# 384-column spatial halves, contiguous transposes, paired causal products and shifted scheduler ranks in a delta-rule, gMLP and rotor kernel

## Chip, cores and metric

The kernel runs on one core of one Trainium2 chip. The metric is the device time of one execution in microseconds (us); less is better. Engines are TensorE (PE, its weight loads PEld), VectorE (DVE), ScalarE (ACT), GpSimd (POOL) and SyncE (SP), whose queue issues all transfers.

## The reference

Three stages follow one another, all in float32, with B = 4 batches, H = 8 heads, S = 768 positions, D = 48.

```python
for t in range(S):                                  # stage 1a: delta rule, k_n = k / |k|
    y[:, :, t] = einsum('bhd,bhde->bhe', q[:, :, t], state)
    v_old = einsum('bhde,bhd->bhe', state, kt)
    state = state + bt * einsum('bhd,bhe->bhde', kt, vt - v_old)
x = y as [B, S, H * D = 384]
u, v = split(maximum(x @ w_in, 0))                  # stage 1b: gMLP, 512 columns each
v_n = (v - mean) / sqrt(var + 1e-6)
v_s = einsum('ts,bsd->btd', w_spatial, v_n) + b_spatial
x = (u * v_s) @ w_out                               # stage 2: rotor
theta = x @ w_theta
y = einsum('ts,bsd->btd', w_tok_r, x * cos(theta)) + einsum(..., w_tok_i, x * sin(theta))
z = x + y;  out = z + maximum(z @ w_ch, 0)
```

## The kernel before

Every instruction is a task with a rank (its priority), a cost in ns on each engine that may run it, and the buffers that it reads and writes. `Plan.run` is a list scheduler: it walks through a modelled time and emits on each engine the task that can start first, among those that can start at once the one of lowest rank. What it emits is the fixed order of each engine's queue. Large matmul groups are tasks marked `big`; in `pe_pick` they fill TensorE while the recurrence waits. Where a gap in the model would let TensorE's clock fall, the planner puts in filler transposes of the identity (`filler`, L529), up to `FILL_K` = 8 for one gap, and 60 once at the start.

Stage 1a. The 48 chunks (4 batches of 12, 64 positions each) are one serial recurrence. `chain(g)` (L831) does, with rank g: products with the state S (`fr`, L854) and a subtraction on VectorE (`rt`, L857); a product with the inverted triangular matrix (`fu`, L866), copied out as U; the update of S (`fs`, L878), copied out; then the output y (`fy`, L902), with rank g + 0.5, added up in `xs` (L913) and stored. `fr`, `fu` and `fy` share one PSUM tile, `ru`, so the next `fr` waits for the add at L913. `jit(g)` (L787) makes the masked product of k and q for a chunk: on PSUM tile `m` for the first 12 chunks, then on `gp` with one mask product of 256 elements on VectorE (L811). The triangular matrices of 8 chunks at a time (a round, six in all) are made by `gram2` and inverted by `invert(r)` (L666): a mask product in place in GX (L678, not in round 0), a 32x32 transpose from GX into `un` (L688), a norm, 30 steps of elimination with a product and an add each (L727, L738), a product with gaT (L741), two more transposes (L744 in place in `un`, L747 back into GX), and small matmuls (L765, L771). There is one buffer of `un`.

Stage 1b. Each float32 matmul of this and the next stage is three (high x high, high x low, low x high parts). For each batch `m_V` projects 128 positions at a time to 512 columns and normalises; `m_U` makes u transposed, 256 positions at a time; `m_S(b, h3, fp)` (L1113) makes the spatial product for 256 positions (h3 of three) and two groups of 128 features, which lie side by side in one PSUM tile: 2 x 18 matmuls of 256 columns. VectorE adds the bias (L1128) and multiplies with u (L1131), 512 elements each, and the tile `gt`, of which there are two, is stored to DRAM (L1133). There are two PSUM tiles `m`. All matmuls of `mm_tasks` carry line 1012. Weights of stage 2 are meanwhile converted and parked in DRAM (`park`, L1181).

Stage 2 opens its PSUM when the recurrence has ended. For each of 24 tiles of 128 positions: reload of the gated product every second tile (`load_g`, L1283: two pieces of 512 columns, split into high and low parts in the single buffers `gh` and `gl`), `X2`, a transpose `T2`, `TH`, sine and cosine, and 36 matmuls of 384 columns (`Y`); the output per batch in `U2` and `O`.

```python
r_gt = ring("w3", "gt", [128, 2, TG], F32, 2)                      # L959
k = max(min(need, FILL_K), min(room, more))                        # L370, fillers for a gap
```

## Time and profile before

| | us |
|---|---|
| median of 3 runs | 736.78 (736.3 to 739.08) |
| profiled execution | 740.0 |
| its span, first to last instruction | 738.2 |
| TensorE busy | 688.6 (93%) |
| VectorE busy | 553.8 (75%) |
| ScalarE busy | 358.6 (49%) |

The span is from the first to the last instruction of the profiled execution, whose own time is a little longer. Busy time is the union of an engine's instructions. [...] The profile's page gives busy time per engine, the same in 40 slices, and the costliest groups of instructions; the trace gives each stretch, group and instruction. After a wait, `<-` names what ended it. Matmuls are pipelined, so the distance between their starts, not the length of one, is what a stream costs.

### The profile page before, as it was taken

To read this page: it belongs to the slowest core of one execution; us is meant where nothing else is said; L and a number is where in the kernel's file an instruction comes from. 1 tells how busy PE (TensorE), PEld (TensorE's weight loads), DVE (VectorE), ACT (ScalarE), POOL (GpSimd) and SP (SyncE) were. 2 spreads that over 40 slices of the span, in tenths; PEclk is the share of its full clock that TensorE was granted. 3 is DMA by queue.
4 is the path that set the end of the run, shared out by engine and by line. 5 is a ranking of instruction groups with operands and counts; after the bars stand their busy time and mean duration, and the time that the engine had idled before them with its cause. 6 is when DMAs were issued, how large, how long until landed. Compare 5 with 4: busy or idle time off the path is not lost. (4 is left out here: it accounts for less than half of the span.)

```text
span 738.2 us, 23758 instructions
## 1 busy us (share of the span) xinstructions
PE 688.6 (93%) x10048; PEld 636.9 (86%) x10048; DVE 553.8 (75%) x1530; ACT 358.6 (49%) x874; POOL 12.4 (2%) x18
## 2 busy tenths in 40 slices
PE   5585988799998999999989999999999999999997
PEld 4575676599886798888889899999999999999997
DVE  7999999959989999857756868776555746574555
ACT  5755484543366762367754764564232423332331
POOL 0010010000010000100000000000000000000000
PEclk9995899879999999999999999999999999999999
DMA  8434634415457535667687543530100011011001
GB/s 300 146 113 125 188 107 127 137 39 154 151 161 213 176 89 160 172 214 230 198 257 273 159 145 128 168 115 30 65 29 28 29 65 30 29 29 65 0 1 65
DMA packets 67786, 90.65 MB, mean 123 GB/s; under 512 B 6624, under 2 KB 46432, under 8 KB 67680
## 3 DMA queue, kind: packets, MB, share of 16 engines
q1 hardware_dynamic: 67680, 89.14, 39.0%
q8 instruction: 79, 1.29, 0.7%
q14 instruction: 27, 0.22, 0.1%
HBM read 66.70 MB, written 22.41 MB: 121 GB/s over the span
## 5 line engine op out<-in xcount | busy, mean ns | idle before, releaser
L1012 PE MATMUL m<-w,vh 128*128 128x256 f32 x576 | 112.5, 294 | 2.7 <-DVE gt L1128 2.7
L1012 PEld LDWEIGHTS m<-w,vh 128*128 128x128 f32 x576 | 90.1, 193 | 6.1 <-DVE gt L1128 3.0
L1012 PE MATMUL y<-wr,xTh 128*128 128x384 f32 x432 | 86.5, 338 | 0.0
L1012 PE MATMUL y<-w,xTl 128*128 128x384 f32 x432 | 84.7, 338 | 0.0
L1012 PE MATMUL m<-w,vl 128*128 128x256 f32 x288 | 81.9, 284 | 0.2 <-DVE vl L943 0.2
L1012 PEld LDWEIGHTS y<-wr,xTh 128*128 128x128 f32 x432 | 75.8, 188 | 0.0
L1012 PEld LDWEIGHTS y<-w,xTl 128*128 128x128 f32 x432 | 75.4, 188 | 0.0
L738 DVE TENSOR_TENSOR un<-un,tmp 128x30 f32<-128x30 f32 (+21 forms) x209 | 60.7, 301 | 1.5
L727 DVE TENSOR_TENSOR tmp<-un 128x30 f32<-128x30 f32 (+21 forms) x209 | 60.5, 300 | 1.5
L1012 PEld LDWEIGHTS m<-w,vl 128*128 128x128 f32 x288 | 55.7, 193 | 0.4 <-DVE vl L943 0.4
L1340 DVE TENSOR_SCALAR bgr<-m 128x384 int32<-128x384 f32 x22 | 12.2, 556 | 56.1 <-PE m L1012 56.1
L497 ACT ACTIVATE U<-ru 128x96 f32<-128x96 f32 x75 | 14.8, 248 | 66.4 <-PE ru L866 49.2
L1012 PE MATMUL m<-xTh,wih 128*128 128x256 f32 x144 | 46.4, 322 | 0.4 <-ACT hv L497 0.4
L1012 PE MATMUL m<-wo,gh 128*128 128x384 f32 x176 | 44.7, 334 | 0.0
L497 ACT ACTIVATE x<-m 128x384 f32<-128x384 f32 x14 | 6.8, 489 | 74.3 <-PE m L1012 74.3
L1012 PE MATMUL m<-xTl,wih 128*128 128x256 f32 x144 | 41.9, 291 | 0.0
L1012 PE MATMUL m<-xTh,wil 128*128 128x256 f32 x144 | 41.7, 290 | 0.0
L1012 PE MATMUL m<-uh,wc 128*128 128x384 f32 x144 | 38.3, 335 | 0.0
L497 ACT ACTIVATE bgr<-bgr 128x384 uint8<-128x384 uint8 x34 | 36.6, 1075 | 0.5
L1012 PE MATMUL m<-wt,xh 128*128 128x384 f32 x132 | 33.8, 337 | 0.0
L1012 PE MATMUL m<-wih,xTh 128*128 128x512 f32 x72 | 33.2, 461 | 0.4 <-ACT xTh L497 0.3
L1354 DVE TENSOR_TENSOR bgr<-x,bgr 128x384 f32<-128x384 f32 x48 | 25.9, 553 | 9.6 <-ACT bgr L497 9.2
(186 smaller groups left out, 1647.0 us busy)
## 6 DMA issues: line engine op xcount, KB each, us to landing
kq<-in_kqT_dram SPq DMA_DIRECT2D x48, 256.0 KB, 3.6
vk<-in_vkn_dram SPq DMA_DIRECT2D x48, 192.0 KB, 3.0
kg<-in_kgT_dram SPq DMA_DIRECT2D x24, 256.0 KB, 3.4
gd<-gt SPq DMA_DIRECT2D x24, 256.0 KB, 3.0
graw<-gd SPq DMA_DIRECT2D x24, 256.0 KB, 2.8
xd<-xs SPq DMA_DIRECT2D x48, 96.0 KB, 2.9
xr<-xd SPq DMA_DIRECT2D x24, 192.0 KB, 3.0
bgr<-in_w_r_dram SPq DMA_DIRECT2D x12, 384.0 KB, 4.5
```

The costliest lines, as they stand in the source:

```text
L497: nc.scalar.activation(out=out, in_=in_, func=func, **kw)
L727: nc.vector.tensor_tensor(out=t3, in0=un.t[:, k:k + 1, 0:k].to_broadcast([128, m, k]), in1=un.t[:, t0:32:st, k:k + 1].to_broadcast([128, m ...
L738: nc.vector.tensor_tensor(out=un.t[:, t0:32:st, 0:k], in0=un.t[:, t0:32:st, 0:k], in1=t3, op=ALU.add)
L1012: mm(out=view(), lhsT=a, rhs=c, start=(start and q == 0 and s_ == 0), stop=(stop and q == tot - 1 and s_ == 2))
L1340: P.add(o_dve(DM), lambda e: nc.vector.tensor_scalar(out=ni.t.bitcast(I32), in0=th(), scalar1=1.0 / TWO_PI, scalar2=None, op0=ALU.mult), [ ...
L1354: P.add(o_tts(DM), lambda e, src=src: eng[e].tensor_tensor(out=src.t, in0=x2.t, in1=src.t, op=ALU.mult), [x2], [src], pr)
```

## The change

- `m_S` takes 384 positions (h of two) and one group of 128 features: 18 matmuls of 384 columns in one PSUM tile, 8 tiles per batch where there were 6. The bias add has 384 elements; the product with u is cut at the borders of the 256-position tiles of u, into pieces of 256 and 128. `gt` has 384 columns and three buffers. The gated product lies in DRAM in pieces of 384 columns; `load_g` reads it in pieces of 256 or, across the border of a half, twice 128, with four buffers, and splits it 256 columns at a time.
- In `invert`, the mask product writes `un` in transposed order and the first transpose is in place and contiguous (not in round 0). The product with gaT writes GX, again in another order, and the second transpose reads GX without a stride along its blocks.
- `jit` from chunk 12 on makes the products of two chunks in one task and masks them with one VectorE instruction of 512 elements.
- S and U have 16 zero columns more, so `fy` loads 64 columns as weights and writes all rows; two memsets of `ru` go, four small ones on GpSimd come.
- `fu` of chunk g is ordered behind `fy` of chunk g - 2.
- At most 4 fillers for one gap. The ranks of four runs of tasks are shifted by fixed pseudo-random offsets (`NUDGE`: seed, first task, last task, size). `STAY` is 0 and does nothing; modelled costs of the transposes are new.

```diff
-FILL_K = 8
+FILL_K = 4
...
+STAY = 0.0
+NUDGE = ((9376, 863, 1113, 0.3), (6411, 2108, 2228, 0.6), (938, 2559, 2679, 0.6), (1081, 1922, 2422, 0.3))
+TRB = 1900.0
+SPER = 6
+GTN = 3
...
+        for k, lo, hi, amp in NUDGE:
+            r = random.Random(k)
+            for t in self.tasks[lo:hi]:
+                t.prio += r.uniform(-amp, amp)
...
-    St = [pools["pa"].tile([128, HP, D], F32, name=f"S{i}") for i in range(2)]
-    Ut = [pools["pa"].tile([128, HP, D], F32, name=f"U{i}") for i in range(2)]
+    St = [pools["pa"].tile([128, HP * D + 16], F32, name=f"S{i}") for i in range(2)]
+    Ut = [pools["pa"].tile([128, HP * D + 16], F32, name=f"U{i}") for i in range(2)]
...
-    r_jp = ring("pa", "jp", [128, HP, CH], F32, JPN)
+    r_jp = ring("pa", "jp", [128, 2 * HP, CH], F32, JPN)
...
         if not cr:
             A([("DVE", d_dve(1024))], lambda e: nc.vector.tensor_tensor(
-                out=gx[:, :, 0:32], in0=gx[:, :, 0:32], in1=mask2.t.unsqueeze(1).to_broadcast([128, 32, 32]), op=ALU.mult),
-              G + [mask2, gg[1], gg[3]], gm2, pr)
-        un = r_un.new()
+                out=un.t.rearrange("p t u -> p u t"), in0=gx[:, :, 0:32], in1=mask2.t.unsqueeze(1).to_broadcast([128, 32, 32]), op=ALU.mult),
+              G + [mask2, gg[1], gg[3]], [un], pr)
+
...
-            nc.vector.transpose(out=un.t, in_=gx[:, :, 0:32].rearrange("p u t -> p t u"))
-
-        A([("DVE", 1900.0)], f1, G + [gg[1], gg[3]] + gm2, [un], pr, crit=cr, port=False)
+            nc.vector.transpose(out=un.t, in_=gx[:, :, 0:32].rearrange("p u t -> p t u") if cr else un.t)
+
+        A([("DVE", 1960.0 if cr else 1180.0)], f1, G + [gg[1], gg[3]], [un], pr, crit=cr, port=False)
...
         A([("DVE", d_dve(1024))], lambda e: nc.vector.tensor_tensor(
-            out=un.t, in0=un.t, in1=gt.t.unsqueeze(1).to_broadcast([128, 32, 32]), op=ALU.mult), [un, gt], ub, pr + 0.05, crit=cr)
+            out=gx[:, :, 0:32].rearrange("p s t -> p t s"), in0=un.t, in1=gt.t.unsqueeze(1).to_broadcast([128, 32, 32]), op=ALU.mult),
+          [un, gt] + ub, gg, pr + 0.05, crit=cr)
         xt = Buf()
-        A([("DVE", 1900.0)], lambda e: nc.vector.transpose(out=un.t.rearrange("p u s -> p s u"),
-                                                           in_=un.t.rearrange("p t s -> p s t")),
-          ub, [xt, un], pr + 0.05, crit=cr, port=False)
-        A([("DVE", 1900.0)], lambda e: nc.vector.transpose(out=gx[:, :, 0:32], in_=un.t), [xt, un], gg, pr + 0.1, crit=cr, port=False)
+        A([("DVE", TRB)], lambda e: nc.vector.transpose(out=un.t.rearrange("p u s -> p s u"), in_=gx[:, :, 0:32]),
+          gg, [xt, un], pr + 0.05, crit=cr, port=False)
+        A([("DVE", 1250.0)], lambda e: nc.vector.transpose(out=gx[:, :, 0:32], in_=un.t), [xt, un], gg, pr + 0.1, crit=cr, port=False)
...
+        elif g % 2 == 0:
-            pj = [lambda: GPt[:, 384:512], lambda: GPt[:, 512:640]]
...
+            jp = jp_b[g] = jp_b[g + 1] = r_jp.new()
+            A(o_pe(2 * JPE), f, [kq_b[g], kq_b[g + 1]], pss + [jp], pr, after=grams if r < 2 else (), act=0.55)
+            A(o_dve(512), lambda e: nc.vector.tensor_tensor(
+                out=jp.t, in0=GPt[:, 256:768].rearrange("p (h t) -> p h t", t=CH), in1=mask.t[:, 0].unsqueeze(1).to_broadcast([128, 8, CH]), op=ALU.mult),
+              [pss[0], mask], [jp], pr, port=False, after=inv0)
...
+        marks[g].order.update(ys_b[-2:-1])
...
-                        lh, rh = s[i:i + D, SB[hp], :], kq.t[i:i + D, 1, hp, :]
+                        lh, rh = s[i:i + D, D * SB[hp]:D * SB[hp] + 64], kq.t[i:i + D, 1, hp, :]
                     else:
-                        lh, rh = u[i:i + 64, UB[hp], :], jp.t[i:i + 64, SB[hp], :]
-                    mm(out=PYv[h][o:o + D, c0:c0 + CH], lhsT=lh, rhs=rh, start=f, stop=w == 1 or UF[hp] > 0, skip_group_check=True)
+                        lh, rh = u[i:i + 64, D * UB[hp]:D * UB[hp] + 64], jp.t[i:i + 64, SB[hp] // 2 * 4 + (g % 2 * 2 if g >= JM else 0) + SB[hp] % 2, :]
+                    mm(out=PYv[h]()[o:o + 64, c0:c0 + CH], lhsT=lh, rhs=rh, start=f, stop=w == 1 or UF[hp] > 0, skip_group_check=True)
...
-    r_gt = ring("w3", "gt", [128, 2, TG], F32, 2)
...
+    r_gt = ring("w3", "gt", [128, HALF], F32, GTN)
...
-    def m_S(b, h3, fp, pr):
+    def m_S(b, h, f, pr):
-        v3 = (lambda: ps.t.rearrange("p (f t) -> p f t", t=TG))
-        t0, t1 = h3 * TG, (h3 + 1) * TG
-        for ff in range(2):
-            f0, f1 = (2 * fp + ff) * 128, (2 * fp + ff + 1) * 128
-            gr = [lambda i=i, f0=f0, f1=f1: (vh_b[b, i].t[:, f0:f1], vl_b[b, i].t[:, f0:f1], ws_h[i].t[:, t0:t1], ws_l[i].t[:, t0:t1])
-                  for i in range(NT)]
-            mm_tasks(ps, lambda ff=ff: v3()[:, ff, :], gr, TG, [[vh_b[b, i], vl_b[b, i], ws_h[i], ws_l[i]] for i in range(NT)],
-                     pr, per=UPER)
-        gt, u, gd = r_gt.new(), uT_b[b, h3], gdram[b][fp][h3]
-        if fp == 0:
-            bs_b[b, h3] = r_bs.new()
-            load(bs_b[b, h3], lambda t=bs_b[b, h3]: t.t, b_sp[:, t0:t1], 131072, pr)
-        bs = bs_b[b, h3]
-        P.add(o_dve(2 * TG), lambda e: nc.vector.tensor_tensor(
-            out=gt.t, in0=v3(), in1=bs.t.unsqueeze(1).to_broadcast([128, 2, TG]), op=ALU.add),
+        t0, f0, f1 = h * HALF, f * 128, (f + 1) * 128
+        gr = [lambda i=i: (vh_b[b, i].t[:, f0:f1], vl_b[b, i].t[:, f0:f1], ws_h[i].t[:, t0:t0 + HALF], ws_l[i].t[:, t0:t0 + HALF])
+              for i in range(NT)]
+        mm_tasks(ps, lambda: ps.t[:, 0:HALF], gr, HALF, [[vh_b[b, i], vl_b[b, i], ws_h[i], ws_l[i]] for i in range(NT)], pr, per=SPER)
+        gt, gd = r_gt.new(), gdram[b][f][h]
+        if f == 0:
+            bs_b[b, h] = r_bs.new()
+            load(bs_b[b, h], lambda t=bs_b[b, h]: t.t, b_sp[:, t0:t0 + HALF], 196608, pr)
+        bs = bs_b[b, h]
+        P.add(o_dve(HALF), lambda e: nc.vector.tensor_tensor(out=gt.t, in0=ps.t[:, 0:HALF], in1=bs.t, op=ALU.add),
-        P.add(o_tts(2 * TG), lambda e: eng[e].tensor_tensor(out=gt.t, in0=gt.t, in1=u.t[:, 2 * fp:2 * fp + 2, :], op=ALU.mult),
-              [u], [gt], pr)
-        stores.add(P.add(dma(262144), lambda e: nc.sync.dma_start(out=gd.t, in_=gt.t), [gt], [gd], pr, extra=2000.0))
+        t = t0
+        while t < t0 + HALF:
+            n = min(t0 + HALF, (t // TG + 1) * TG) - t
+            u = uT_b[b, t // TG]
+            P.add(o_tts(n), lambda e, u=u, t=t, n=n: eng[e].tensor_tensor(
+                out=gt.t[:, t - t0:t - t0 + n], in0=gt.t[:, t - t0:t - t0 + n], in1=u.t[:, f, t % TG:t % TG + n], op=ALU.mult),
+                  [u], [gt], pr)
+            t += n
+        stores.add(P.add(dma(196608), lambda e: nc.sync.dma_start(out=gd.t, in_=gt.t), [gt], [gd], pr, extra=2000.0))
...
+        for h in range(2):
+            for f in range(KF):
+                m_S(b, h, f, pr)
...
-        for f in range(KF // 2):
-            raw, gd = r_gr.new(), gdram[b][f][h3]
-            P.add(dma(262144), lambda e, raw=raw, gd=gd: nc.sync.dma_start(out=raw.t, in_=gd.t), [gd], [raw], pr, extra=LOADLAT)
-            split(raw, lambda raw=raw: raw.t, 2 * TG, gh, lambda f=f: gh.t[:, 2 * f:2 * f + 2], gl, lambda f=f: gl.t[:, 2 * f:2 * f + 2], pr)
+        t0 = h3 * TG
+        for f in range(KF):
+            raw = r_gr.new()
+            t = t0
+            while t < t0 + TG:
+                h = t // HALF
+                n, gd = min(t0 + TG, (h + 1) * HALF) - t, gdram[b][f][h]
+                P.add(dma(512 * n), lambda e, raw=raw, gd=gd, t=t, n=n, h=h: nc.sync.dma_start(
+                    out=raw.t[:, t - t0:t - t0 + n], in_=gd.t[:, t - h * HALF:t - h * HALF + n]), [gd], [(raw, t > t0)], pr, extra=LOADLAT)
+                t += n
+            split(raw, lambda raw=raw: raw.t, TG, gh, lambda f=f: gh.t[:, f], gl, lambda f=f: gl.t[:, f], pr)
```

## Rows read from the trace of the kernel before

**Rows 1.** The page's 40 slices of the span, busy tenths of VectorE.
```profile
DVE  7999999959989999857756868776555746574555
```

**Rows 2.** Stretches: us; busy by engine (instructions); granted clock (PEclk); DMA share, GB/s.
```profile
0.00:276.00 276.00, 234.00 (x5761) 200.74 (x5762) 249.60 (x817) 157.27 (x433) 10.39 (x14) 0.91 0.49 148
140.00:144.00 4.00, 1.93 (x6) 0.97 (x6) 3.93 (x6) 0.14 (x2) 0.00 (x0) 0.99 0.43 158
144.00:160.00 16.00, 15.78 (x275) 14.18 (x277) 8.87 (x26) 7.30 (x18) 2.25 (x2) 0.58 0.20 55
232.00:244.00 12.00, 8.30 (x263) 6.87 (x263) 11.93 (x42) 7.87 (x22) 0.00 (x0) 0.95 0.74 229
276.00:460.00 184.00, 180.51 (x2698) 163.49 (x2697) 134.62 (x366) 103.36 (x235) 2.04 (x4) 0.99 0.63 194
384.00:394.00 10.00, 7.30 (x46) 6.98 (x45) 7.69 (x16) 5.48 (x8) 0.00 (x0) 0.83 1.03 382
460.00:738.00 278.00, 274.07 (x1593) 272.69 (x1591) 169.56 (x349) 97.99 (x207) 0.00 (x0) 1.00 0.16 51
```

**Rows 3.** TensorE in order of time: start us, us, instruction [idle before <-releaser].
```profile
235.09 0.45 PE L854 MATMUL ru<-S,kq 48*64 48x48 f32 x16 [1.53 <-DVE xs L913]
```

**Rows 4.** VectorE, then TensorE, in order of time, 140 to 146 us.
```profile
141.93 2.10 DVE L744 STREAM_TRANSPOSE un<-un 128x1024 f32<-128x1024 f32 x1
...
144.22 0.68 PE L854 MATMUL ru<-S,kq 48*64 48x48 f32 x16 [0.96 <-DVE xs L913]
```

**Rows 5.** TensorE in order of time: first spatial product, then stage two.
```profile
432.65 0.40 PE L1012 MATMUL m<-w,vh 128*128 128x256 f32 x2
...
438.39 0.40 PE L1012 MATMUL m<-w,vh 128*128 128x256 f32 x2
...
472.99 1.72 PE L1012 MATMUL y<-wr,xTh 128*128 128x384 f32 x9
...
474.55 1.72 PE L1012 MATMUL y<-w,xTl 128*128 128x384 f32 x9
```

**Rows 6.** Line 1128 alone, by stretch: VectorE busy us (instructions).
```profile
0.00:276.00 276.00, 4.10 (x6) 0.91 0.49 148
...
375.00:460.00 85.00, 7.49 (x11) 0.98 0.59 193
```

**Rows 7.** Groups by form: instruction, shapes xcount | busy us, mean ns | idle before.
```profile
L943 DVE TENSOR_TENSOR w<-gt,w 128x384 fp32r<-128x384 f32 x12 | 6.5, 552 | 0.6 <-ACT w L497 0.5
...
L943 DVE TENSOR_TENSOR wil<-vl,wih 128x256 fp32r<-128x256 f32 x12 | 4.9, 417 | 0.1
...
L913 DVE TENSOR_TENSOR xs<-xs,ru 128x128 f32<-128x128 f32 x44 | 12.3, 280 | 2.2 <-ACT xs L497 2.0
...
L1128 DVE TENSOR_TENSOR gt<-m,bs 128x512 f32<-128x512 f32 x24 | 16.4, 686 | 10.7 <-PE m L1012 5.5 <-DMA bgr<-in_w_i_dram 3.0 <-DMA bs<-in_b_sp_dram 1.8
...
L811 DVE TENSOR_TENSOR jp<-gp,mask 128x256 f32<-128x256 f32 x36 | 15.0, 415 | 2.2 <-PE gp L803 2.2
```

**Rows 8.** DMA issues: KB each, median us from issue to landing.
```profile
graw<-gd SPq DMA_DIRECT2D x24, 256.0 KB, 2.8
```

**Rows 9.** TensorE in order of time, at 388 us.
```profile
388.39 0.51 PE L1012 MATMUL m<-w,vh 128*128 128x256 f32 x2 [2.70 <-DVE gt L1128]
```

**Rows 10.** Groups by form: the three large transposes of an inversion.
```profile
L688 DVE STREAM_TRANSPOSE un<-GX 128x1024 f32<-128x1024 f32 x6 | 11.8, 1964 | 4.4 <-PE gp L765 4.3 <-ACT GX L497 0.2
...
L744 DVE STREAM_TRANSPOSE un<-un 128x1024 f32<-128x1024 f32 x6 | 13.0, 2160 | 0.0
...
L747 DVE STREAM_TRANSPOSE GX<-un 128x1024 f32<-128x1024 f32 x6 | 7.5, 1243 | 0.0
```

**Rows 11.** Line 811 alone, by stretch.
```profile
0.00:276.00 276.00, 15.63 (x46) 0.91 0.49 148
```

**Rows 12.** Groups by form: weight loads of 48 and of 64 columns.
```profile
L902 PEld LDWEIGHTS ru<-jp,U 64*48 64x48 f32 x768 | 24.8, 129 | 0.0
...
L866 PEld LDWEIGHTS ru<-rt,GX 64*64 64x64 f32 x768 | 16.7, 142 | 12.5 <-DVE rt L857 5.2 <-issue 1.0 <-DVE un L738 0.9
```

More of the change, by code (lines that the diff above doesn't have):

```diff
@@ L58 @@
 HAM_DN = 0.34
-HAM_T = .42
+HAM_T = 0.42
 SLIDE = 3413
@@ L75 @@
 JM = 12
+YM = 0
+YP = 0.5
 JPE = 290
@@ L254, in pe_pick @@
             return c
+        if STAY and self.warm and self.mode == 1 and c[1].big:
+            o = [x for x in l if x[1].mode == 1 and x[0] <= s0 + STAY]
+            if o:
+                return min(o, key=lambda x: (x[0], x[1].prio, x[1].uid))
         if best is None or c[1].big:
@@ L546 @@
     pool("ps_a", space=PSUM)
-    gdram = [[[Buf(tile_=pools["dram"].tile([128, 2, TG], F32, name=f"gd{b}{f}{h}")) for h in range(S // TG)]
-              for f in range(KF // 2)] for b in range(B)]
+    gdram = [[[Buf(tile_=pools["dram"].tile([128, HALF], F32, name=f"gd{b}{f}{h}")) for h in range(2)]
+              for f in range(KF)] for b in range(B)]
     def single(pl, name, shape, dtype=F32):
@@ L572 @@
     PSb = [Buf(tile_=PSt) for _ in range(2)]
-    r_y, PYv = r_ru, [RUt[:, h, 256:448] for h in range(2)]
-    RUz = Buf(tile_=RUt)
     for b_ in PSb:
@@ L608 @@
         A([("DVE", 300.0)], lambda e, q=q: nc.vector.memset(PSt[q:q + 32, :, 0:2 * D], 0.0), (), PSb, -31, port=False, part=q)
-        A([("DVE", 600.0)], lambda e, q=q: nc.vector.memset(RUt[q:q + 32, :, 256:448], 0.0), (), [RUz], -31, port=False, part=q)
+    for i in range(2):
+        A([("POOL", 100.0)], lambda e, i=i: nc.gpsimd.memset(St[i][:, HP * D:], 0.0), (), SS[i], -30 + i, port=False)
+        A([("POOL", 100.0)], lambda e, i=i: nc.gpsimd.memset(Ut[i][:, HP * D:], 0.0), (), UU[i], -30 + i, port=False)
     kq_b, vk_b, jp_b = {}, {}, {}
@@ L805, in jit @@
-        jp = jp_b[g] = r_jp.new()
-        A(o_pe(JPE), f, [kq], pss + [jp], pr, after=grams if r < 2 else (), act=0.55)
-        for h in (0, 1) if jm else (None,):
-            n = HP if h is None else 2
-            src = (lambda h=h: GPt[:, 384:640] if h is None else pj[h]())
-            dst = (lambda h=h: jp.t if h is None else jp.t[:, 2 * h:2 * h + 2])
-            A(o_dve(64 * n), lambda e, n=n, src=src, dst=dst: nc.vector.tensor_tensor(
-                out=dst(), in0=src().rearrange("p (h t) -> p h t", t=CH), in1=mask.t[:, 0].unsqueeze(1).to_broadcast([128, n, CH]), op=ALU.mult),
-              [pss[h or 0], mask], [(jp, bool(h))], pr, port=False, after=inv0)
+            for w in (0,) if jm else (0, 1):
+                kq = kq_b[g + w]
+                for hp in (0, 1, 2, 3):
+                    for a in (0, 64):
+                        o, c = 64 - a if UF[hp] else a, 128 * w + SB[hp] % 2 * CH
+                        mm(out=pj[SB[hp] // 2]()[o:o + 64, c:c + CH], lhsT=kq.t[a:a + D, 0, hp, :], rhs=kq.t[a:a + D, 1, hp, :], start=True, stop=True)
@@ new lines, in jit @@
+        if jm:
+            jp = jp_b[g] = r_jp.new()
+            A(o_pe(JPE), f, [kq_b[g]], pss + [jp], pr, after=grams if r < 2 else (), act=0.55)
+            for h in (0, 1):
+                A(o_dve(128), lambda e, h=h: nc.vector.tensor_tensor(
+                    out=jp.t[:, 4 * h:4 * h + 2], in0=pj[h]().rearrange("p (h t) -> p h t", t=CH), in1=mask.t[:, 0].unsqueeze(1).to_broadcast([128, 2, CH]), op=ALU.mult),
+                  [pss[h], mask], [(jp, bool(h))], pr, port=False, after=inv0)
+        elif g % 2 == 0:
+            jp = jp_b[g] = jp_b[g + 1] = r_jp.new()
[3 more added lines that the diff above has]
+              [pss[0], mask], [jp], pr, port=False, after=inv0)
@@ L882, in chain @@
             for h in (0, 1):
-                A(o_cpp(96), lambda e, h=h: copy(e, two(sn)[0:112, h], PSt[0:112, h, 0:2 * D]), [PSb[h]], [ssn[h]], pr, crit=True, port=False)
-        py = r_y.new()
+                A(o_cpp(96), lambda e, h=h: copy(e, sn[0:112, 2 * D * h:2 * D * h + 2 * D], PSt[0:112, h, 0:2 * D]), [PSb[h]], [ssn[h]], pr, crit=True, port=False)
+        if g < YM:
+            pys = [r_m.new(), r_m.new()]
+            PYv = [lambda p=p: p.t[:, 0:192] for p in pys]
+        else:
+            pys = [r_ru.new()]
+            PYv = [lambda h=h: RUt[:, h, 256:448] for h in range(2)]
         yc = (lambda w, hp: (w, 64 * (SB[hp] % 2)) if UF[hp] else (YF[hp], 128))
```

42 lines of the change are left out of this document (18 added, 24 removed).

## The prediction

> **What bounds the kernel now.** I read the page first: its slices show DVE (VectorE) at nine tenths or more in most of the first 16, and TensorE full over the second half [rows 1]. A mean over the span therefore says little, and the second view cuts it [rows 2]. Up to 276 us DVE is busy 249.6 of 276 us, TensorE 234.0; from 276 to 460 TensorE is busy 180.5 of 184 and DVE has a quarter of its time free; from 460 on TensorE is busy 274 of 278. So the time is that at which TensorE can no longer run out of work, plus TensorE's work from there on.
>
> Where that point lies is seen in the same view. From 232 to 244 us TensorE is busy only 8.3 of 12 us while DVE is busy 11.9: the projections of batch 1 wait for the recurrence, and the recurrence for DVE. One of PE's rows there holds a wait of 1.53 us for the DVE add at L913 [rows 3]. After about 276 us such lack is gone, since the spatial product of batch 1 is then open. Up to there I count DVE time, behind it TensorE time. [...]
>
> **Spatial halves, the matmuls.** Per batch 216 matmuls of 256 columns become 144 of 384: 864 become 576. From 432.65 to 438.39 us stand 48 matmuls of 256 columns, 16 times the same three, 119.6 ns each; the 9 of 384 columns from 472.99 to 474.55 take 173.3 ns each [rows 5]. 864 x 119.6 = 103.3 us, 576 x 173.3 = 99.8 us: 3.5 us less, 0.88 per batch. Columns streamed are the same; only a fixed part of some 12 to 14 ns goes with each of the 288 matmuls saved. Of the 24 bias adds that close the old tiles, 6 lie before 276 us and 18 behind [rows 6], so three batches lie on the TensorE-bound part: **-2.6 us**. Were batch 0 on the path too it would be -3.5.
>
> **Spatial halves, the rest.** Each PSUM tile is now 18 matmuls (3.1 us) rather than 36 of 256 columns (4.3 us), so the two buffers turn faster; DVE needs 0.55 us for a bias add of 384 and 0.42 + 0.28 for the two products with u, 1.25 us together [rows 7], and in the TensorE-bound part it has the room. Per batch DVE had 6 x (0.686 + 0.686) = 8.2 us and gets 8 x 1.25 = 10.0: +1.8. Only batch 0's lies in the DVE-bound part: **+1.8 us**. DMA issues on SP: 24 stores become 32, 24 reloads become 64, 12 bias loads become 8, 44 issues more; behind a reload that waits for its buffer stand the other reloads and the output stores. The splits of the reloads are twice as many and half as long, 2 x 0.42 for 0.69 us on DVE: 24 x 0.15 = 3.6 us more, under a DVE that is 61% busy after 460 [rows 2, 7]. I cost both at nothing; without that cover the second tile of a pair would start late, at most the 2.8 us of one landing [rows 8].
>
> **The stall at 385 us.** TensorE sits 2.70 us for the bias add L1128, and of the ten us from 384 on it is busy 7.3 at a mean clock of 0.83 [rows 2, 9]: with the 0.17 x 10 = 1.7 us of clock that is 4.4 us. A third gt buffer and smaller units make this stall less likely, the shorter PSUM tile makes it more likely. Bounds -4.4 and, if the wait comes twice, +2.7; I take half of the first: **-2 us**.
>
> **Contiguous transposes.** Reading with a stride costs: L688 (strided in, plain out) 1964 ns against L747 (plain in) 1243, so 0.72 us. Storing with a stride costs less: L744, strided on both sides, 2160, which is 0.20 more than L688 [rows 10]. In rounds 1 to 5 the first transpose loses its strided read; in all six the second does. Ten of these eleven lie before 276 us. What moves is the stride: the mask product (L678) and the product with gaT (L741) now store with it. No row shows such a store by a product; the bounds are 0 and 0.72, and I take the 0.20 of the transpose's own store, the nearest row. Ten times 0.52: **-5.2 us** (-7.2 to 0). The mask product also needs `un` now. Before, it needed only GX and could run ahead of the matmuls of the preceding round, which read `un`; now it waits for them, and rt, vk and jp of the chunks queue behind it on DVE, and with rt the recurrence on TensorE. L688 waits there already, so nothing that waits is new; I add nothing. The bound is that the product no longer fills that wait, some 1.2 us (a plain transpose's time) in each of five rounds.
>
> [...]
>
> **Paired causal products.** From chunk 12 on one mask product of 512 elements (686 ns) replaces two of 256 (415 ns): 0.144 us a pair. 46 of the 60 instructions, 24 of them of the early kind, lie before 276 us, so 11 pairs: **-1.6 us** [rows 7, 11]. The matmuls are the same; the pair needs kq of the next chunk, which is loaded three chunks ahead. Widening S and U as weights from 48 to 64 columns: a weight load of 48 takes 129 ns and one of 64 takes 142 [rows 12], overlapped except for a part; 13 ns x 16 matmuls x the 14 chunks behind 276 us = 2.9 us at most, 0 at least; small matmuls of four groups overlap, so I take **+0.5**. The two RUt memsets go; they run while the first loads are still on their way.
>
> **Order.** Fillers per gap fall from 8 to 4, u(g) must follow y(g-2), and four runs of ranks are shifted by up to 0.3 or 0.6 of a chunk. Counting tasks along the code, they are about chunks 18 to 25, the projections and spatial products of batches 1 to 3, and some of the parked conversions. Neither sign follows from the rows. What is there to win or lose is the low clock at 144 to 160 (6.7 us, first rival) and the idle from 232 to 244; I take 0.
>
> **The sum.** DVE part -5.2 - 1.6 + 1.8 = -5.0; DVE is busy 90% there, and I take 0.9 of it, -4.5. TensorE part -2.6 - 2.0 + 0.5 = -4.1. Together -8.6. The profiled execution took 740.0 us (span 738.2), so 731.4; it lies 3.2 us over the median of the runs (736.78), and against that the forecast is 728.2, given as **728.0 us**.
>
> **Rivals.**
> 1. *The clock window goes as well* (721.3). From 144 to 160 us a mean clock of 0.58 loses 0.42 x 16 = 6.7 us [rows 2]. It begins where L744 holds back the add at L913, for which PE waits 0.96 us [rows 4]. [...] For it: the wait is the transpose's own. Against: PE waited for other splits there too, and the new order may open such a gap elsewhere. Chance 0.22.
> 2. *The stride is moved, not removed* (734). Stores cost what reads cost, -5.2 becomes 0, DVE's part is +0.2 and the whole -3.9 (-1.9 if the stall at 385 also stays): 733 to 735. Chance 0.20.
> 3. *Slower, by the clock* (741.4). From 232 to 244 us filler transposes (L529) hold the level while matmuls are lacking, a mean of 0.95 [rows 2, 3]; with at most four a gap it falls earlier. One more window like 144 to 160 costs 6.7 us, less than the gain; two cost 13.4, and 728 + 13.4 = 741.4. Two windows where TensorE is otherwise busy are the point from which this decides. Against it: shorter DVE work narrows the very gaps that fillers stand in. Chance 0.12.
>
> That big spatial tasks (6 x 173 = 1.04 us, before 0.72) stand longer ahead of the recurrence costs nothing by itself: behind 276 us TensorE has other work, and after 375 us, when the recurrence has ended, 11 of 24 spatial tiles are still to come [rows 6].
>
> **How the numbers follow.** The forecast has 0.46, with its own range 723 to 733 from the bounds of the transposes (+-2), the stall and the small terms. The range 718 to 738 takes in rivals 1 and 2 and leaves out most of rival 3. A measurement of this kernel tells about 0.5% from no change, 3.7 us, so 733.1 is the border: faster 0.46 + 0.22 and a little of rival 2 = 0.71; within 0.17; slower 0.12.
>
> **What would show it.** Right: spatial matmuls of 384 columns at 173 ns; L688's and L744's successors at about 1.25 and 1.45 us and both products 0.2 us longer; the start of batch 1's spatial product about 5 us earlier; no wait of PE for the bias add over 1 us. Wrong: products 0.7 us longer; a granted clock under 0.9 in new stretches after 160 us; PE idle after 276 us; waits of PE for reloads after 460. If the gain is far over 9 us, the order did it and not the terms above.

## The result, and the profile after

| | before | after |
|---|---|---|
| runs, median (lowest to highest) | 736.75 us (736.3 to 739.08) | 726.58 us (725.02 to 727.55) |
| profiled execution, its span | 740.0, 738.2 us | 725.02, 722.9 us |
| mean granted clock of the span | 0.965 | 0.981 |

The ratio is 0.9832 (95% interval 0.9801 to 0.9864): faster, and 1.4 us from the forecast of 728.0. The size of the gain is less sure than the time: the two medians alone give 0.9862, 10.2 us less; the ratio stands for 12.4 us, and a second pair of medians further down gives 12.9. The forecast was 8.6. A right time can still come from wrong terms, so the profile is read step by step as it was before.

The page's slices first (forty per line, busy tenths; PEclk is the granted clock in tenths of full speed), and under them the clock's line of the kernel before.

```profile
PE   4585889899999999999999999999999999999997
DVE  6999989989999989996767868977466745674555
PEclk9995899999999999999999999999999999999999
```

```profile
PEclk9995899879999999999999999999999999999999
```

VectorE is still full in most of the first 16 slices [rows 1], and TensorE over the second half: the bound has not moved. In the clock's line the 5 and the 8 from 54 to 90 us are left; the 8 and the 7 that the kernel before had in its eighth and ninth slice (129 to 166 us) are gone. In steps of 1 us the clock reads 0.50 or 1.00, and something between only where it changes: in the kernel before 0.50 from 144 to 157 us and 1.00 from 158 to 170.

The stretches of after (us; busy by engine with instructions; granted clock; DMA share, GB/s), among them those of [rows 2]:

```profile
0.00:276.00 276.00, 233.89 (x5761) 197.72 (x5765) 252.03 (x815) 155.70 (x426) 10.34 (x18) 0.95 0.51 153
140.00:144.00 4.00, 3.80 (x42) 2.69 (x43) 3.79 (x16) 0.96 (x4) 0.00 (x0) 0.88 0.76 224
144.00:160.00 16.00, 15.53 (x436) 14.03 (x438) 12.57 (x29) 8.63 (x25) 2.31 (x2) 1.00 0.35 97
232.00:244.00 12.00, 11.90 (x208) 9.24 (x207) 11.94 (x43) 8.86 (x23) 0.00 (x0) 1.00 0.50 163
276.00:460.00 184.00, 182.70 (x2502) 164.06 (x2493) 147.50 (x434) 110.43 (x258) 2.04 (x4) 1.00 0.66 201
384.00:394.00 10.00, 10.00 (x62) 8.99 (x61) 8.05 (x25) 7.64 (x21) 0.00 (x0) 1.00 0.93 297
```

Three holes of before have closed: 144 to 160 us (clock 0.58 then, 1.00 now), 232 to 244 (TensorE busy 8.30 then, 11.90 now) and 384 to 394 (busy 7.30 at 0.83 then, 10.00 at 1.00 now). VectorE, which the forecast had relieved in the first 276 us, is busy there 252.0 us, against 249.6 before. TensorE's idle time up to 276 us has not shrunk, 42.1 us for 42.0: what the hole at 232 us gave stands idle elsewhere.

Cut into stretches of 2 us, the same view splits a span into TensorE's idle time, the time lost to a lower clock (busy time x (1 - clock)) and what is left, its work at full clock:

| profiled execution | span | idle | lost to clock | work |
|---|---|---|---|---|
| before | 738.2 | 49.6 | 21.5 | 667.2 |
| after | 722.9 | 47.6 | 9.4 | 665.9 |

Of the 15.3 us between the two profiles, 12.1 are clock, 2.0 idle and 1.3 work. These are one execution each, and that of the kernel before was one of its slower ones (740.0 us, its median 736.75), so 15.3 is on the high side.

The inversion's large steps by form (instruction, shapes xcount | busy us, mean ns | idle before). L694 is the mask product, L704 the first transpose, L757 the product with gaT, L761 and L763 the second and third transpose:

```profile
L761 DVE STREAM_TRANSPOSE un<-GX 128x1024 f32<-128x1024 f32 x6 | 12.1, 2024 | 0.1
L757 DVE TENSOR_TENSOR GX<-un,gaT 128x1024 f32<-128x1024 f32 x6 | 12.0, 2000 | 0.1
L694 DVE TENSOR_TENSOR un<-GX,mask 128x1024 f32<-128x1024 f32 x5 | 10.0, 2003 | 8.0 <-PE gp L781 8.0
L763 DVE STREAM_TRANSPOSE GX<-un 128x1024 f32<-128x1024 f32 x6 | 7.4, 1232 | 0.0
L704 DVE STREAM_TRANSPOSE un<-un 128x1024 f32<-128x1024 f32 x5 | 6.2, 1240 | 0.0
```

The first transpose did fall from 1964 to 1240 ns, but the second, which still stores with a stride, only from 2160 to 2024 [rows 10], and both products now take 2.00 us. A round became longer.

The other VectorE forms touched by the change, and the wider weights:

```profile
L1152 DVE TENSOR_TENSOR gt<-m,bs 128x384 f32<-128x384 f32 x32 | 17.7, 552 | 10.6 <-PE m L1040 9.5 <-DMA bs<-in_b_sp_dram 1.0
L1158 DVE TENSOR_TENSOR gt<-gt,uT 128x256 f32<-128x256 f32 x32 | 13.3, 415 | 0.2
L1158 DVE TENSOR_TENSOR gt<-gt,uT 128x128 f32<-128x128 f32 x32 | 9.1, 283 | 0.1
L832 DVE TENSOR_TENSOR jp<-gp,mask 128x512 f32<-128x512 f32 x18 | 12.2, 680 | 0.0
L929 PEld LDWEIGHTS ru<-jp,U 64*64 64x64 f32 x768 | 26.5, 141 | 0.0
```

They are as forecast: 552, 415, 283 and 680 ns, and a weight load of 141 ns for 129 [rows 7, 12]. From 376 to 460 us the list of TensorE's waits is empty: none for L1152 is left. The spatial matmuls in order of time (start us, us, instruction):

```profile
429.75 0.51 PE L1040 MATMUL m<-w,vh 128*128 128x384 f32 x2
...
431.31 0.51 PE L1040 MATMUL m<-w,vh 128*128 128x384 f32 x2
```

Nine start in 431.31 - 429.75 = 1.56 us, 173.3 ns each, the pitch of [rows 5]; the mean length of one in the page is 349 ns. Where batch 1's spatial product stands (TensorE's instructions that write `m` from `vh`, 215 to 330 us), before and after:

```profile
L1012 PE MATMUL m<-w,vh x144: 277/283/387, 271.7 to 320.3; 128*128 128x256 f32 x144
```

```profile
L1040 PE MATMUL m<-w,vh x96: 331/334/446, 252.7 to 300.6; 128*128 128x384 f32 x96
```

It starts 19 us earlier, where about 5 had been forecast.

### The profile page after: what moved, and what is told of

Same layout as the page of the kernel before. It is cut to its first block, busy times and chain, and to the rows that moved or that the text cites. A ratio compares the mean times of both kernels' runs of the same rounds, so it can differ in the third digit from the quotient of the medians.

```text
span 722.9 us, 23312 instructions
## 1 busy us (share of the span) xinstructions
PE 675.3 (93%) x9750; PEld 619.1 (86%) x9750; DVE 560.8 (78%) x1603; ACT 356.3 (49%) x877; POOL 12.4 (2%) x22
## 4 chain that ended last, share of the span: by engine, by line
PE 54%; DVE 1%; ACT 0%; issue 0%
PE m L1040 29%; PE y L1040 22%; PE m L1351 1%; PE ru L929 1%; PE ru L887 0%; PE ru L875 0%; PE s L900 0%; PE gp L820 0%; PE gp L781 0%; PE gp L787 0%; DVE bgm L964 0%; DVE ul L971 0%; DVE uf L1427 0%; ACT bgr L513 0%; DVE bgm L962 0%
## 5 line engine op out<-in xcount | busy, mean ns | idle before, releaser
L1040 PE MATMUL m<-w,vh 128*128 128x384 f32 x384 | 102.9, 349 | 0.0
L1040 PEld LDWEIGHTS m<-w,vh 128*128 128x128 f32 x384 | 66.2, 188 | 2.9
L1040 PE MATMUL m<-w,vl 128*128 128x384 f32 x192 | 64.4, 336 | 0.0
L754 DVE TENSOR_TENSOR un<-un,tmp 128x30 f32<-128x30 f32 (+22 forms) x209 | 60.8, 302 | 1.5
L743 DVE TENSOR_TENSOR tmp<-un 128x30 f32<-128x30 f32 (+23 forms) x209 | 60.5, 301 | 1.5
L1040 PE MATMUL m<-xTh,wih 128*128 128x256 f32 x144 | 44.9, 312 | 1.5 <-ACT hv L513 1.5
L513 ACT ACTIVATE x<-m 128x384 f32<-128x384 f32 x22 | 10.6, 482 | 70.2 <-PE m L1040 70.2
L1040 PEld LDWEIGHTS m<-w,vl 128*128 128x128 f32 x192 | 36.0, 188 | 0.0
L929 PE MATMUL ru<-jp,U 64*64 64x64 f32 x768 | 33.2, 229 | 0.0
```

The costliest lines, as they stand in the source:

```text
L513: nc.scalar.activation(out=out, in_=in_, func=func, **kw)
L743: nc.vector.tensor_tensor(out=t3, in0=un.t[:, k:k + 1, 0:k].to_broadcast([128, m, k]), in1=un.t[:, t0:32:st, k:k + 1].to_broadcast([128, m ...
L754: nc.vector.tensor_tensor(out=un.t[:, t0:32:st, 0:k], in0=un.t[:, t0:32:st, 0:k], in1=t3, op=ALU.add)
L929: mm(out=PYv[h]()[o:o + 64, c0:c0 + CH], lhsT=lh, rhs=rh, start=f, stop=w == 1 or UF[hp] > 0, skip_group_check=True)
L1040: mm(out=view(), lhsT=a, rhs=c, start=(start and q == 0 and s_ == 0), stop=(stop and q == tot - 1 and s_ == 2))
```

## The experiments

Two theories stood after this. By the first (B in the expectations), the terms of the sum were about right and the transposes' loss was hidden somewhere. By the second (A), the transposes cost time, and the order in which the planner now lays the work on the engines paid for it. To tell them apart a duration must be changed under a fixed order and the order under fixed durations, since the planner makes another order as soon as a modelled cost or a task changes. "Same order" below means that every engine's queue holds its instructions in the same sequence as in the changed kernel. Another order is more than a sequence: the planner also decides anew which of two engines takes some tasks, and how many fillers stand in the gaps. Each ratio is to the kernel before on the same chip, whose medians were 739.01, 738.29 and 738.79 us in the three groups of runs.

**The offsets taken away** (`e1_plain`), all else of the change kept:

```diff
-NUDGE = ((9376, 863, 1113, 0.3), (6411, 2108, 2228, 0.6), (938, 2559, 2679, 0.6), (1081, 1922, 2422, 0.3))
+NUDGE = ()
```

> The changed kernel with the rank offsets taken out (an empty list), all else as it is. Instructions and their shapes are the same but for fillers; only the order in the queues differs. Theory A, the order did most of it (the low clock at 144 to 160 us and the stall at 385 us are gone by the order): 730 to 736 us, with a stretch of low clock back. Theory B, the durations did it (fewer matmuls, paired products): 725 to 728, as with the offsets.

734.21 us, ratio 0.9949 (0.9924 to 0.9973). Without four lists of pseudo-random numbers most of the gain is gone. The low clock after 144 us is gone here too (the clock's slices are those of the changed kernel, figure for figure), so that does not need the offsets; what differs most is idle time, and there are 138 fillers for 149. Two stretches of it:

```profile
130.00:276.00 146.00, 136.20 (x3257) 114.33 (x3255) 137.75 (x403) 79.20 (x225) 6.29 (x6) 0.99 0.49 146
375.00:460.00 85.00, 80.39 (x508) 75.96 (x507) 62.81 (x173) 53.66 (x106) 0.14 (x2) 0.98 0.66 207
```

and the same two of the changed kernel:

```profile
130.00:276.00 146.00, 139.07 (x3305) 117.11 (x3308) 134.39 (x396) 79.11 (x220) 6.09 (x6) 0.99 0.49 147
375.00:460.00 85.00, 85.00 (x539) 82.30 (x538) 65.28 (x178) 55.73 (x114) 0.14 (x2) 1.00 0.67 206
```

TensorE is busy 2.9 and 4.6 us less. Of the second, 3.0 us are one wait, for a conversion of another stage (TensorE's waits from 376 to 460 us: waiter, releaser, us, times, longest):

```profile
PE y L1040 <- ACT xTh L513: 3.0, 1, 3.0
```

So with three gt buffers there is no wait for the bias add here either, but in this order another wait of the same size stands in its place.

**Other random numbers** (`e2_seeds`): the same four runs of tasks and sizes, other seeds.

```diff
-NUDGE = ((9376, 863, 1113, 0.3), (6411, 2108, 2228, 0.6), (938, 2559, 2679, 0.6), (1081, 1922, 2422, 0.3))
+NUDGE = ((1, 863, 1113, 0.3), (2, 2108, 2228, 0.6), (3, 2559, 2679, 0.6), (4, 1922, 2422, 0.3))
```

> The changed kernel with seeds 1, 2, 3, 4 in place of the four given, same runs of tasks and sizes: another order of the same work. Theory A (order): off the changed kernel by 2 us or more, in either direction, 724 to 737. Theory B (durations): within 1.5 us of it, 725 to 728. Together with e1 this says how far an arbitrary order scatters.

735.03 us, 0.9959 (0.9926 to 0.9992). This one other set of seeds is worth nothing over no offsets at all; the set of the change is worth 8 to 10 us over either neighbour.

**The old access patterns under the new order** (`e3_oldpat`): products and transposes read and store as in the kernel before, modelled costs and so the order stay.

```diff
-                out=un.t.rearrange("p t u -> p u t"), in0=gx[:, :, 0:32], in1=mask2...
+                out=gx[:, :, 0:32], in0=gx[:, :, 0:32], in1=mask2...
...
-            nc.vector.transpose(out=un.t, in_=gx[:, :, 0:32].rearrange("p u t -> p t u") if cr else un.t)
+            nc.vector.transpose(out=un.t, in_=gx[:, :, 0:32].rearrange("p u t -> p t u"))
...
-            out=gx[:, :, 0:32].rearrange("p s t -> p t s"), in0=un.t, in1=gt.t...
+            out=un.t, in0=un.t, in1=gt.t...
...
-                ...transpose(out=un.t.rearrange("p u s -> p s u"), in_=gx[:, :, 0:32]),
+                ...transpose(out=un.t.rearrange("p u s -> p s u"), in_=un.t.rearrange("p t s -> p s t")),
```

> The changed kernel with the access patterns of the three transposes and the two products of an inversion as before, and with every engine's order as in the changed kernel: only durations differ. The changed profile shows products of 2.00 us (before 1.22) and transposes of 1.24, 2.02 and 1.23 (before 1.96, 2.16 and 1.24), so this takes 0.69 us of VectorE out of rounds 1 to 5 and 0.64 out of round 0, 4.1 in all. Theory C, VectorE sets the pace until about 276 us: 723 to 724.5. Rival D, with this order TensorE is the limit there already: 726 to 727. The prediction's own pricing (stride moved for 0.20) would have it 5 us slower, 731.

721.21 us, 0.9774 (0.9728 to 0.9821): the fastest kernel of the study, 5.4 us under the changed kernel's first median and 4.2 under its second (below). By the ratios, each taken on its own chip, it is 0.5% under the second, 3.7 us; 4.1 less VectorE time had been expected to give 723 to 724.5. Its groups, to set beside the five of after:

```profile
L761 DVE STREAM_TRANSPOSE un<-un 128x1024 f32<-128x1024 f32 x6 | 13.1, 2175 | 0.0
L704 DVE STREAM_TRANSPOSE un<-GX 128x1024 f32<-128x1024 f32 x6 | 11.9, 1976 | 0.2 <-ACT GX L513 0.2
L763 DVE STREAM_TRANSPOSE GX<-un 128x1024 f32<-128x1024 f32 x6 | 7.4, 1237 | 0.0
L757 DVE TENSOR_TENSOR un<-un,gaT 128x1024 f32<-128x1024 f32 x6 | 7.3, 1223 | 0.1
L694 DVE TENSOR_TENSOR GX<-GX,mask 128x1024 f32<-128x1024 f32 x5 | 6.1, 1212 | 0.0
```

Mask product and first transpose: 1212 + 1976 = 3.19 us here, 2003 + 1240 = 3.24 in the change; that stride was moved and nothing else. Product with gaT and second transpose: 1223 + 2175 = 3.40 here, 2000 + 2024 = 4.02 in the change, 0.63 more. The old transpose had both its strides in one instruction, which costs 2175 - 1237 = 0.94 us over a plain one; the new pair pays 2000 - 1223 = 0.78 for one and 2024 - 1232 = 0.79 for the other. With the third transpose a round takes 7.82 us the old way and 8.50 the new, 0.68 more in rounds 1 to 5 and 0.6 in round 0: 4.0 us more VectorE time, and the kernel is about 4 us slower for it (3.7 and 4.3 by the ratios). The two profiled executions differ by only 2.2 us of span, since that of the old patterns was its slowest and that of the change its fastest: 4.7 us less idle time, 1.8 less work, 4.4 more lost to the clock.

The added wait for `un`, in both kernels (VectorE's waits up to 300 us), first the changed kernel, then this one:

```profile
DVE un L694 <- PE gp L781: 8.0, 4, 3.0
```

```profile
DVE U L519 <- PE ru L887: 4.6, 3, 2.3
DVE rt L878 <- PE ru L875: 3.6, 3, 2.7
```

The mask product waits 8.0 us in the change. Where it can run ahead, the same idle time, 4.6 + 3.6 = 8.2 us, stands before the recurrence's own steps that follow it. So the wait stands either way; needing `un` added nothing to it.

**The spatial halves alone** (`e4_halves`): the kernel before with only that part.

```diff
-    def m_S(b, h3, fp, pr):
+    def m_S(b, h, f, pr):
...
-    r_gt = ring("w3", "gt", [128, 2, TG], F32, 2)
+    r_gt = ring("w3", "gt", [128, HALF], F32, GTN)
...
-        for h3 in range(S // TG):
-            for fp in range(KF // 2):
-                m_S(b, h3, fp, pr)
+        for h in range(2):
+            for f in range(KF):
+                m_S(b, h, f, pr)
```

> The kernel before with the spatial halves alone (384-column matmuls, three gt buffers, the reload in four pieces), nothing else. By the matmuls alone (theory B) 3.5 us less than before: 732 to 734. With theory A the order that follows from it adds up to 5 us in either direction, and the stretch of low clock at 144 to 160, which lies before the first spatial product, stays: 731 to 738.

733.54 us, 0.9936 (0.9906 to 0.9967), about 4.7 us. The planner makes another order here too, so this is halves and an order together. With three gt buffers TensorE still waited for the bias add, and for other steps, late in the kernel (its waits, 376 to 460 us):

```profile
PE m L1014 <- DVE gt L1126: 1.2, 1, 1.2
PE m L1325 <- ACT x L499: 0.9, 1, 0.9
PE m L1014 <- DVE xl L1333: 0.8, 1, 0.8
PE m L1014 <- ACT xh L499: 0.7, 1, 0.7
```

**The changed kernel once more** (`after_again`), for the group with the next three.

> The changed kernel as it is, on the same chip as the three kernels beside it, as their yardstick: 0.983 of the kernel before.

725.41 us, 0.9824 (0.9776 to 0.9872), as the first time.

**The paired mask product split in two** (`e6_splitmask`), same order:

```diff
-            A(o_dve(512), lambda e: nc.vector.tensor_tensor(
-                out=jp.t, in0=GPt[:, 256:768]..., in1=mask..., op=ALU.mult), ...
+            def fm(e):
+                for w in (0, 1):
+                    nc.vector.tensor_tensor(out=jp.t[:, 4 * w:4 * w + 4], in0=GPt[:, 256 + 256 * w:512 + 256 * w]..., in1=mask..., op=ALU.mult)
+
+            A(o_dve(512), fm, ...
```

> The changed kernel with each paired mask product done as two instructions of 256 elements, every queue's order kept. 18 times 2 x 0.415 - 0.680 = 0.15 us, 2.7 us more on VectorE, some 1.7 of it before 276 us. Theory C (VectorE sets the pace there, as the run with the old access patterns said): 1.5 to 2.5 us over the changed kernel. Rival D (a few tenths of a us between recurrence steps are lost in waits): within 1 us of it.

727.46 us, 0.9853 (0.9799 to 0.9906), 2.05 us over the changed kernel beside it. The intervals overlap, so this is agreement with 18 x (2 x 415 - 680) = 2.7 us of VectorE time rather than proof.

**Each spatial matmul of 384 columns as 256 + 128** (`e7_splitmm`), same order:

```diff
-                        mm(out=view(), lhsT=a, rhs=c, ...)
+                        for x0, x1 in cuts or ((0, n),):
+                            mm(out=view()[:, x0:x1], lhsT=a, rhs=c[:, x0:x1], ...)
...
-        mm_tasks(ps, lambda: ps.t[:, 0:HALF], gr, HALF, ..., per=SPER)
+        mm_tasks(ps, lambda: ps.t[:, 0:HALF], gr, HALF, ..., per=SPER, cuts=((0, 256), (256, 384)))
```

> The changed kernel with each spatial matmul of 384 columns done as one of 256 and one of 128 into the same tile, every queue's order kept: same columns, 576 matmuls more. From 119.6 ns for 256 columns and 173.3 for 384 the fixed part is some 13 ns a matmul, so 576 x 13 = 7.4 us more on TensorE, 5.6 of it in batches 1 to 3. Theory E, TensorE is the bound from batch 1's spatial product on: 5 to 8 us over the changed kernel (more if 128 columns are too few to cover a weight load). Rival F, TensorE has slack there: under 2 us.

753.29 us, 1.0204 (1.0153 to 1.0254): 27.9 us more than the changed kernel beside it, far more than expected. TensorE in order of time:

```profile
439.98 0.63 PE L1042 MATMUL m<-w,vh 128*128 128x256 f32 x4
...
440.67 0.63 PE L1042 MATMUL m<-w,vh 128*128 128x256 f32 x4
```

Three pairs take 0.69 us, 231 ns a pair for 173.3. With 119.6 ns for the 256 columns [rows 5], 128 columns with a weight load of their own cost some 111 ns, not the 66 to which the pitch of the wider ones leads (53 ns by columns and a fixed 13). The price does not go on falling with the columns down to 128. The run still settles its point: 576 x 57.7 ns = 33.2 us of TensorE time were added in the same order, and 27.9, or 84%, came out in the time. By that share the 3.5 us that the halves save on TensorE are worth 2.9.

**The kernel before in another order** (`e8_before_order`): no task changed, only offsets on its ranks, picked for an early end of the kernel's own plan. The planner moves 6 tasks from VectorE to ScalarE by it and puts in 176 fillers for 159.

```diff
+NUDGE = ((6939, 1000, 1500, 0.3), (214, 700, 1200, 0.6), (1756, 0, 250, 0.6), (7986, 0, 500, 0.3), (6475, 2300, 2800, 0.3))
...
+        for k, lo, hi, amp in NUDGE:
+            r = random.Random(k)
+            for t in self.tasks[lo:hi]:
+                t.prio += r.uniform(-amp, amp)
```

> The kernel before with rank offsets of its own and nothing else: five runs of tasks, seeds kept one after another where the planner's modelled end came earlier (728.8 to 719.4 us in its own model, while the offsets of the change lower the changed kernel's modelled end from 716.1 to 709.9). No instruction is changed. Theory A (order): 3 to 9 us under the kernel before, and less idle time and less time at the low clock in the records. Theory B (durations): within 2 us of it.

729.72 us, 0.9879 (0.982 to 0.9939): 8.6 us from order alone, most of what the whole change brought. Of the 9.4 us between the profile of the kernel before and this one, 8.1 are clock. Two of its stretches, to be read against [rows 2]:

```profile
140.00:160.00 20.00, 19.00 (x517) 16.19 (x505) 17.97 (x52) 10.78 (x28) 1.89 (x2) 1.00 0.42 121
384.00:394.00 10.00, 10.00 (x62) 9.34 (x62) 6.17 (x13) 5.84 (x11) 0.00 (x0) 1.00 1.01 371
```

Both holes close: the low clock after 144 us, and the stall at 385 us, here with the old units of 512 and two gt buffers.

**Old patterns, measured costs for the planner, offsets of their own** (`e9_best`): the patterns of the third experiment, with 1.96 and 2.15 us as the modelled costs of the strided transposes and ten runs of offsets picked for that plan; the mask product may also be placed ahead of `un` again, as in the kernel before.

```diff
-        A([("DVE", 1960.0 if cr else 1180.0)], f1, ...
+        A([("DVE", 1960.0)], f1, ...
...
-        A([("DVE", TRB)], ...
+        A([("DVE", 2150.0)], ...
```

> The changed kernel with the inversion of the kernel before (0.69 us a round less on VectorE), the measured costs of its transposes in the planner, and rank offsets of its own, kept where the planner's modelled end came earlier (729.9 to 713.2 us). The kernels run so far took 10 to 15 us more than a modelled end with true prices. By theory A (order) and theory C (VectorE early on): 722 to 728 us; it beats the changed kernel only if the new order is as good as its.

722.73 us, 0.9776 (0.9735 to 0.9818): as fast as the third experiment, not faster.

**The weights of 48 columns again** (`e10_narrow`), same order:

```diff
-                        lh, rh = s[i:i + D, D * SB[hp]:D * SB[hp] + 64], ...
+                        lh, rh = s[i:i + D, D * SB[hp]:D * SB[hp] + D], ...
```

> The changed kernel with S and U again 48 columns wide as weights of the output product, the rows it no longer writes cleared once at the start, every queue's order kept. The changed profile shows weight loads of 141 ns, before 129. If they are hidden under matmuls of other groups: within 1 us of the changed kernel. If they stand on TensorE's path: 13 ns x 16 x 48 = 10 us at the very most, 2 to 3 us of it behind 276 us; the prediction took 0.5.

727.6 us, 0.9839 (0.9784 to 0.9894). The loads are back at 127 ns, and nothing is gained by it.

**Old patterns and narrow weights together** (`e11_oldpat_narrow`), same order, the two edits shown above.

> The same order once more, with the old access patterns of the inversion and 48-column weights together. With the old patterns alone 0.9774 of the kernel before was measured, with the changed kernel 0.983. If the two edits add up: that less what 48 columns give, 0.974 to 0.978. A second measurement of the old patterns' gain: at least 0.3% under the changed kernel if theory C holds, none if that was the chip.

723.78 us, 0.9785 (0.9742 to 0.9828). Against its neighbour with the new patterns 3.8 us less: the second pair that differs in the patterns alone, after 721.21 against 725.41. Each difference is within the overlap of its two intervals, so neither pair is proof by itself; both have the same sign and the size of the 4.0 us of VectorE time. The profiled executions of this second pair differ by 0.6 us only (that of `e10_narrow` was its fastest): 3.4 us less idle time against 3.1 more lost to the clock.

**The change's offsets on another plan** (`e12_truecost`): the kernel of `e9_best` with the four offsets of the change as they stand.

```diff
-NUDGE = ((4545, 500, 620, 0.6), (8357, 2559, 2809, 0.3), ...
+NUDGE = ((9376, 863, 1113, 0.3), (6411, 2108, 2228, 0.6), (938, 2559, 2679, 0.6), (1081, 1922, 2422, 0.3))
```

> As the first kernel of this call (inversion as before, measured costs), but with the offsets of the change as they stand. By durations alone it would beat the changed kernel by 4 us (721). Theory A: offsets fit one plan only; with other costs they are an arbitrary order, whose modelled end is 729.9, so 733 to 744 us.

738.53 us, 0.9992 (0.9963 to 1.0021), 15.8 us slower than `e9_best` beside it, with the same tasks and durations; 13 tasks have gone from VectorE to ScalarE, and there are fewer fillers. The clock carries most of it, and the low clock after 144 us is back (for `e9_best` the clock from 140 to 160 us is 1.00):

```profile
0.00:130.00 130.00, 94.73 (x2326) 82.06 (x2327) 113.51 (x404) 73.60 (x196) 4.51 (x12) 0.82 0.51 155
130.00:276.00 146.00, 137.25 (x3178) 115.87 (x3176) 127.96 (x389) 81.08 (x224) 5.67 (x6) 0.89 0.48 139
```

```profile
140.00:160.00 20.00, 17.20 (x432) 13.77 (x430) 14.12 (x36) 9.79 (x28) 1.89 (x2) 0.64 0.39 112
```

The fillers of the two, first `e9_best`, then `e12_truecost`:

```profile
L545 PE MATMUL gp<-ident 128*128 128x128 f32 x165 | 24.6, 301 | 0.1
L545 PE MATMUL ru<-ident 128*128 128x128 f32 x61 | 9.3, 284 | 0.0
```

```profile
L545 PE MATMUL gp<-ident 128*128 128x128 f32 x109 | 17.4, 322 | 0.0
L545 PE MATMUL ru<-ident 128*128 128x128 f32 x34 | 5.0, 282 | 0.0
```

The split of the first table for the kernels that differ mainly in order, with the number of fillers and their busy time:

| profiled execution | span | idle | lost to clock | work | fillers |
|---|---|---|---|---|---|
| before | 738.2 | 49.6 | 21.5 | 667.2 | 159, 23.4 |
| after | 722.9 | 47.6 | 9.4 | 665.9 | 149, 22.7 |
| offsets away | 731.7 | 53.7 | 12.5 | 665.5 | 138, 19.8 |
| other seeds | 736.2 | 51.5 | 17.7 | 667.0 | 151, 22.4 |
| old patterns, same order | 720.7 | 42.9 | 13.8 | 664.1 | 149, 22.7 |
| before, other order | 728.8 | 44.0 | 13.4 | 671.3 | 176, 27.6 |
| old patterns, own offsets | 720.9 | 34.2 | 10.8 | 675.8 | 226, 33.9 |
| the same, the change's offsets | 741.3 | 49.9 | 31.6 | 659.8 | 143, 22.4 |

TensorE's work at full clock runs from 660 to 676 us, both ends in the last two rows. Fillers count as busy, and at full clock they are 32.9 and 21.4 us of it there, 11.5 of the 16.0 us; the other 4.5 were not followed up. The same holds for the idle time, which runs from 34 to 54 us: a filler only takes its place. Idle time and fillers together are 66 to 74 us in all eight rows, and the lowest is the kernel that had 4.0 us of VectorE time taken away in the same order. The loss to the clock runs from 9 to 32 us. So an order sets above all what is lost to the clock, and not by the number of fillers alone: 149 go with 9.4 us in the changed kernel, 143 with 31.6 in the last.

Each row is one execution. Over all of them the mean granted clock was 0.981 to 0.986 in the four of `e9_best`, 0.976 to 0.981 in the eight of the changed kernel, 0.958 to 0.976 in 45 of the kernel before and 0.944 to 0.958 in the ten of `e12_truecost`.

## Why the prediction was right, and where it was not

The time was right by luck: two terms failed in opposite directions, each by some 9 us, and the forecast missed by 1.4.

- **Contiguous transposes, -5.2: wrong, in sign too.** The failing step is the price of a product's strided store, taken at the transpose's 0.20 us. It costs 0.78, near the upper bound of 0.72 and just beyond it. Moreover the second transpose kept its strided store, and with the strided read gone gave back 0.14 us, not 0.72: it was put at about 1.45 us and takes 2.02. The step read 0.20 as the price of a strided store in general; it was the price of a second stride in an instruction that already pays for one. The measured term is +4.0 us of VectorE time, and by two pairs of runs some +4 in the time. The prediction had named this sign of being wrong, products 0.7 us longer. The second rival had it right that stores cost what reads cost (2.00 us for 1.22 by a product's store, 1.98 for 1.24 by a transpose's read) but brought the term only up to 0, where the true one is above 0.
- **Order, 0: wrong.** Order is worth 8 to 10 us either way: offsets away or changed in the new kernel, +7.6 to +9.6 by either median of it and +8.6 to +10.0 by the ratios; an order alone on the old one, -8.6. It also moved batch 1's spatial product, which starts at 252.7 us with the offsets, at 258.2 and 261.9 with them away or changed, and at 256.9 for 271.7 in `e8_before_order`, where no duration changed. The first rival named the low clock after 144 us as what could be won, and it was won. It is no property of the 2.10 us transpose, as that rival had it: with the old transposes `e8_before_order` has a clock of 1.00 from 140 to 160 us and `e12_truecost` 0.64. The holes at 232 and 385 us closed too, but all idle time together fell by 2.0 us only. The third rival's earlier fall of the clock from 232 to 244 us did not come: 12 fillers stand there for 22, TensorE is busy 11.90 us for 8.30, and the clock is 1.00 for 0.95. The sentence at the end, that a gain far over 9 us would mean order, looked for the sign in the wrong place: order had done it within 9 us.
- **Spatial halves, -2.6: right in mechanism and size.** 173.3 ns held, and the share of TensorE time that reaches the end was 84% by the split matmuls, so 2.9 us. The halves alone gave 4.7, with an order of their own.
- **Evacuation, +1.8:** durations as forecast; no run priced it by itself.
- **Stall at 385 us, -2: gone, but no run shows that the third buffer did it.** The halves alone, with three buffers, still lost 1.2 us to the bias add and 2.4 to three other steps; without the offsets a wait of 3.0 us for a conversion stood there; with another order and two buffers it was gone.
- **Paired products, -1.6:** the run that split them again was 2.05 us slower, not apart from 0 by the intervals.
- **Wider weights, +0.5:** not seen. The load takes 12 ns longer, and undoing it gave nothing. The overlap of small matmuls that the term counted on is there: 16 of L854, with a mean length of 234 ns, take 0.45 us together [rows 3].
- **The added wait for `un`, 0:** right. Where the product could run ahead, the wait of 8.0 us stood before the next steps, 8.2 us long.
- **The cover named for the reloads and stores** held: TensorE is busy 182.70 of 184 us from 276 to 460, and after 460 its one wait in the list is for the split of `ul`, none for a reload:

```profile
PE m L1040 <- DVE ul L971: 0.8, 1, 0.8
```

Put together from the runs: halves -3, pairs -2, transposes +4, weights 0, which leaves about -1 (the evacuation's +1.8 was not priced); the remaining 9 of the 10.2 us between the medians are order (12 if the gain is the 12.9 of the second pair). That remainder is a difference, not a measurement. `e1_plain` and `e2_seeds` give 7.6 to 10.0 for the offsets alone, and `e8_before_order` shows 8.6 for an order on the kernel before.

Open: which of the four runs of offsets does it, and what the limit of four fillers and the ordering of `fu` behind `fy` bring by themselves. No run held the sequence and changed the fillers, so their share in what an order is worth is not shown. The new order with two gt buffers was not tried.

## What to carry to other kernels

When the order of a statically planned kernel moves with every edit, a difference of one per cent says nothing on the edit: hold the order fixed and change the duration, or hold the durations and try several orders, and read idle time, fillers and lost clock apart from work. On VectorE here a stride that left one instruction and entered another cost as much there (0.74 us off the first transpose, 0.79 onto the mask product), and two strides that shared one instruction were cheaper than one each in two (0.94 us for 0.78 + 0.79). Offsets found for one plan are part of that plan; after the next edit they have to be found again.
